# An attention and gated feed-forward kernel: the first queries and keys by SyncE and ScalarE as f32, x in column halves, one global order

## The chip, the cores and the metric

The kernel runs on one core of a Trainium2 chip. The metric is device time in microseconds for one launch. Before the change it is 263.78 us, the median of three runs (263.61 to 264.4).

## The reference

Causal attention over 4 batches, 8 heads, 768 tokens and 64 features a head. Heads 0, 2 and 6 attend to all earlier tokens; the other five attend to the first 4 tokens and the last 64. Its output, laid out as 3,072 tokens by 512 features, is x. Then a gated feed-forward block with a gated residual:

```python
scores = (q @ k.T) / 8                  # per batch and head
scores = where(mask[head], scores, -1e9)
a = exp(scores - max); a = a / (sum(a) + 1e-9)
x = concat_heads(a @ v)                 # (3072, 512)
g = x @ w_gate                          # (3072, 1536)
ffn = (gelu(g) * (x @ w_val)) @ w_out   # (3072, 512)
out = x + sigmoid(x @ w_res) * ffn
```

All inputs and the output are f32. The kernel multiplies in f16 and sums in f32.

## The kernel before

**Tiling.** The 24 token tiles of 128 go through in six chunks of four tiles (`CHUNKS`); a chunk may hold the end of one batch and the start of the next. For each chunk:
- queries and keys come into `qks`, cast to f16 by DMAs that GpSimd issues, and are turned so that features lie on partitions (`qT`, `kT`): on TensorE for chunks 0 and 1 (`loads_rows`, L824 transposes, L835 copies out of PSUM), by DMA transposes on SyncE for the others (`loads_natural`);
- four head pairs get scores on TensorE (L1012, two heads side by side on 64 partitions each; L1103 for the four sink tokens), exp on ScalarE (L1028, L1110), a mask on VectorE (L1064), the product with the values (`va`, and `vs`, the values shifted by 64 tokens; L1136, L616), and division by the row sum (L1190, L1201, L1203), which writes x as f32 (`xtok`) and f16 (`x`);
- x is turned into `xT` (L1225 on TensorE, or a DMA transpose L1216), then gate and value products with `wg` and `wv`, gelu, and `hT`; for half of the features of chunks 1 to 5 with seven products of sub-blocks in place of eight (`fast`, L1361, L1365);
- `wr` gives the residual gate (tanh on ScalarE), `wo` the output, again with seven products in place of eight (`output_fast`, L1494); gate times product goes to `otile` (L1518). For chunks 1 to 4 x is stored first (L1443) and `otile` added to it by an accumulating DMA on GpSimd (L1522); for chunks 0 and 5 x is added on the chip (L1528, L1568) and the tile stored.

Chunk 0 is done in two halves of two tiles each. Its keys and queries of tokens 0 to 255 and of tokens 256 to 511 are the first things that the kernel needs.

**Tile modes of TensorE.** A matmul uses the whole array, or half of its columns (64 output partitions, two at a time, L617 and L824), or half of its rows (scores, L1012), or a quarter (sinks, L1103).

**Order.** `PLAN` holds a list of task numbers for each of the five engines and a buffer number for each tile. `Graph.schedule` walks the five lists through a model of durations; each engine takes only the head of its own list. PSUM banks are given by kind of use (`P_ps`: which banks a kind may have, and how many at once). Where the model's TensorE has nothing ready, it puts in a filler, a matmul of a zero tile `blank` that nobody reads (L1578); fillers are dropped once the first gate product has been placed. `assign_waits` and `emit` then write semaphores and instructions; an engine runs its instructions strictly in the order written.

**Buffers.** x has two f32 buffers of four tiles by 512 columns (`P_x`); `hT` has one.

## Time and profile before

| | |
|---|---|
| time, median of three runs | 263.78 us (263.61 to 264.4) |
| span of the profiled execution | 261.9 us |
| median less that span | 1.88 us |
| TensorE busy, granted clock | 253.3 us (97%), 0.998 |
| VectorE, ScalarE, GpSimd busy | 202.2, 169.0, 107.7 us |
| first scores start, last turn of x in chunk 0 ends | 10.34, 27.35 us |
| last matmul ends | 257.13 us |
| bytes moved by DMA | 33.18 MB, 127 GB/s over the span |

The span runs from the first to the last instruction of the profiled execution; the page gives no other time for that execution, so what lies around the span is taken as the difference to the median. A group's row reads: line, engine, operation, out<-in, count, busy time and mean of one, idle time before. In the stage table each engine has its busy time, with its number of instructions behind it. A busy TensorE is not TensorE at its peak, since each matmul's row covers its pipeline too; the starts of consecutive rows tell how fast matmuls really follow each other.

### The profile page before, as it was taken

To read this page: it belongs to the slowest core of one execution; us is meant where nothing else is said; L and a number is where in the kernel's file an instruction comes from. 1 tells how busy PE (TensorE), PEld (TensorE's weight loads), DVE (VectorE), ACT (ScalarE), POOL (GpSimd) and SP (SyncE) were. 2 spreads that over 40 slices of the span, in tenths; PEclk is the share of its full clock that TensorE was granted. 3 is DMA by queue.
4 is the path that set the end of the run, shared out by engine and by line. 5 is a ranking of instruction groups with operands and counts; after the bars stand their busy time and mean duration, and the time that the engine had idled before them with its cause. 6 is when DMAs were issued, how large, how long until landed. Compare 5 with 4: busy or idle time off the path is not lost.

```text
span 261.9 us, 8109 instructions
## 1 busy us (share of the span) xinstructions
PE 253.3 (97%) x3436; PEld 181.4 (69%) x3436; DVE 202.2 (77%) x443; ACT 169.0 (65%) x303; POOL 107.7 (41%) x146
## 2 busy tenths in 40 slices
PE   7899999999999999999999999999999998999992
PEld 5568655458577477667578577689687677788891
DVE  2587449788888987868988788978687986678974
ACT  2488537795676997467896566896465994564511
POOL 8899918970061964243998330001110040010032
PEclk9999999999999999999999999999999999999999
DMA  7999999999989999999999999607940029060003
GB/s 67 162 186 191 196 191 194 183 170 153 168 226 136 154 138 143 209 178 129 128 93 110 151 199 130 204 5 116 228 104 1 3 22 137 12 80 4 3 22 141
DMA packets 102068, 33.18 MB, mean 127 GB/s; under 512 B 88720, under 2 KB 97168, under 8 KB 102032
## 3 DMA queue, kind: packets, MB, share of 16 engines
q0 software_dynamic: 74704, 18.88, 82.4%
q1 hardware_dynamic: 27040, 13.52, 26.0%
q8 instruction: 27, 0.44, 0.8%
q10 hardware_dynamic: 288, 0.26, 0.3%
q14 instruction: 9, 0.07, 0.1%
HBM read 29.36 MB, written 10.49 MB: 152 GB/s over the span
## 4 chain that ended last, share of the span: by engine, by line
PE 93%; DMA 2%; DVE 1%; issue 1%; POOL 1%; DVEq 0%; POOLq 0%
PE ps L616 47%; PE ps L617 33%; PE ps L1012 6%; DMA qks<-in_q_dram 2%; PE ps L1136 2%; PE ps L1578 2%; PE ps L1225 2%; PE ps L824 1%; PE ps L1103 1%; POOL qks L678 1%; DVE otile L1518 0%; DVE otile L1528 0%; DVE xtok L1203 0%; DVE ea L1064 0%; DVE rcp L1190 0%
## 5 line engine op out<-in xcount | busy, mean ns | idle before, releaser
L1522 POOL DMA_DIRECT2D out_dram<-otile x16 | 14.9, 966 | 87.9 <-DVE otile L1518 65.8
L678 POOL DMA_DIRECT2D qks<-in_k_dram x37 | 31.4, 892 | 31.7 <-DMA kT<-qks 24.3
L616 PE MATMUL ps<-xT,wg 128*128 128x512 f16 (+1 forms) x172 | 38.7, 337 | 0.0
L1291 ACT ACTIVATE gact<-ps 128x512 f16<-128x512 f32 x38 | 21.9, 596 | 22.9 <-PE ps L616 14.8
L1293 DVE SCALAR_TENSOR_TENSOR hT<-gact,ps 128x512 f16<-128x512 f16 x38 | 25.9, 686 | 12.5 <-PE ps L616 6.7
L616 PE MATMUL ps<-xT,wv 128*128 128x512 f16 (+1 forms) x160 | 35.3, 334 | 0.0
L678 POOL DMA_DIRECT2D qks<-in_q_dram x37 | 31.0, 867 | 6.8 <-PE ps L824 6.8
L1365 DVE TENSOR_TENSOR ps<-ps,otile 128x256 f32<-128x256 f32 x60 | 25.0, 430 | 6.3 <-PE ps L617 2.6
L678 POOL DMA_DIRECT2D va<-in_v_dram x24 | 24.3, 1021 | 0.0
L1028 ACT ACTIVATE ea<-ps 128x1024 f16<-128x1024 f32 (+2 forms) x24 | 21.5, 917 | 3.9 <-PE ps L1012 3.7
L1383 ACT ACTIVATE gact<-ps 128x512 f16<-128x512 f32 x30 | 16.5, 594 | 10.4 <-PE ps L616 6.0
L616 PEld LDWEIGHTS ps<-xT,wg 128*128 128x128 f16 x172 | 16.6, 98 | 9.5 <-DVE hT L1293 0.4
L616 PEld LDWEIGHTS ps<-xT,wv 128*128 128x128 f16 x160 | 15.3, 98 | 10.6 <-issue 0.4
L1390 DVE SCALAR_TENSOR_TENSOR hT<-gact,ps 128x512 f16<-128x512 f16 x30 | 19.5, 682 | 3.3 <-PE ps L616 1.8
L617 PE MATMUL ps<-xT,wv 128*64 128x512 f16 (+1 forms) x168 | 20.8, 350 | 0.0
L616 PE MATMUL ps<-wo,hT 128*128 128x256 f16 (+1 forms) x114 | 18.8, 296 | 0.0
L1494 DVE TENSOR_TENSOR otile<-otile,ps 128x256 f32<-128x256 f32 x33 | 13.5, 418 | 6.7 <-PE ps L616 3.4
L1203 DVE TENSOR_TENSOR xtok<-ps,rcp 128x512 f32<-128x512 f32 (+1 forms) x28 | 17.1, 610 | 1.4 <-DVE rcp L1190 0.5
L1462 ACT ACTIVATE srs<-ps 128x512 f32<-128x512 f32 x22 | 13.2, 598 | 7.7 <-PE ps L617 6.5
L617 PE MATMUL ps<-xT,wg 128*64 128x512 f16 (+1 forms) x144 | 17.4, 344 | 0.0
L1012 PE MATMUL ps<-qT,kT 64*128 64x64 f16 (+4 forms) x391 | 16.6, 213 | 0.0
L1361 ACT ACTIVATE ps<-ps 128x256 f32<-128x256 f32 x25 | 9.2, 369 | 10.6 <-PE ps L617 6.9
(174 smaller groups left out, 597.8 us busy)
## 6 DMA issues: line engine op xcount, KB each, us to landing
out_dram<-xtok SPq DMA_DIRECT2D x4, 1024.0 KB, 5.3
out_dram<-otile POOLq DMA_DIRECT2D x16, 256.0 KB, 4.9
va<-in_v_dram POOLq DMA_DIRECT2D x24, 128.0 KB, 8.5
qks<-in_q_dram POOLq DMA_DIRECT2D x32, 64.0 KB, 5.2
qks<-in_k_dram POOLq DMA_DIRECT2D x32, 64.0 KB, 7.6
wv<-in_moe_w_val_dram POOLq DMA_DIRECT2D x3, 512.0 KB, 10.0
wg<-in_moe_w_gate_dram POOLq DMA_DIRECT2D x3, 512.0 KB, 8.1
wo<-in_moe_w_out_dram POOLq DMA_DIRECT2D x4, 384.0 KB, 19.6
```

The costliest lines, as they stand in the source:

```text
L616: return e.matmul(o, lhsT=lhsT, rhs=rhs, **k)
L617: return [e.matmul(o[h:h + 64], lhsT=lhsT[:, h:h + 64], rhs=rhs, **k) for h in (0, 64)][-1]
L678: return G.add(eng, issue, lambda e: e.dma_start(out_ap(), in_ap), deps, prio, bufs=bufs, dma=cost, name=name, grp=grp)
L1012: return [e.matmul(at(scr)[:, oo:oo + w], lhsT=side(BB, qb, low, 1)[half, k0:k0 + 128], rhs=side(BB, qb, low, 0)[half, qq:qq + w], start=T ...
L1028: return e.activation(out=o, in_=i_, func=AF.Exp, scale=SM_SCALE)
L1203: t2 = G.add("dve", c_dve(2 * n * 64), lambda e: e.tensor_tensor(out=xview(), in0=avv(0, DHEAD), in1=scale(), op=ALU.mult), [t1] + xdeps, ...
L1291: ta = G.add("act", c_act(512), (lambda gb=gb, ga=ga, gw=gw: lambda e: e.activation(out=at(ga)[:, :], in_=at(gb)[:, gw], func=AF.Gelu))(), ...
L1293: th = G.add("dve", c_dve(512), (lambda vb=vb, ga=ga, f=f, vw=vw: lambda e: e.scalar_tensor_tensor(out=hv(f), in0=at(ga)[:, :], scalar=0.5 ...
L1365: return G.add("dve", c_dve(256), lambda e: e.tensor_tensor(out=at(ps)[:, o], in0=at(ps)[:, BL], in1=at(es)[:, 0:256], op=ALU.add), deps, ...
L1383: ta = G.add("act", c_act(512), (lambda x=x, ga=ga, both=both: lambda e: e.activation(out=two(at(ga)[:, :]), in_=both(x), func=AF.Gelu))() ...
L1390: th = G.add("dve", c_dve(512), (lambda x=x, f=f, ga=ga, both=both: lambda e: e.scalar_tensor_tensor(out=two(hv(f)), in0=two(at(ga)[:, :]) ...
L1522: t = G.add("pool", 1.0, (lambda ot=ot, r0=r0: lambda e: e.dma_start(out[r0:r0 + 128, :], at(ot)[:, :], accum_op=ALU.add))(), ends + [stor ...
```

## The change

**Loads.** Queries and keys of tokens 0 to 255 no longer come as f16 through GpSimd. SyncE and ScalarE issue eight DMAs of 128 tokens by four heads as f32, into the space of `hT`, which is not in use yet; even heads first, then odd ones. TensorE turns them as f32, 16 transposes of 128 by 128 in place of 32 half transposes, with an f32 identity that VectorE makes there (`wide`), and the copies out of PSUM make f16 of them. GpSimd builds the masks first and then issues the keys of tokens 256 to 511.

**x.** Three half buffers of four tiles by 256 columns in place of two whole ones. The stores of x for chunks 1 to 4 become two each; the additions of x on the chip become two of 256 columns.

**PSUM.** Any use may have any bank or any aligned pair of banks; caps and kinds are gone. The lanes of `fast` are buffers of their own.

**Order.** `PLAN` is one list for all engines; letters say on which of several engines a task runs; `w15` means 15 fillers. There is no model of durations in the program any more. A filler is left out where no bank is free of other engines' reads. The extra edges between tasks that only shaped the order (`order=`) are gone. DMA semaphores are shared by DMAs that follow each other.

```diff
-    P_x = Pool(many("xtok", 2, [128, 4, D_MODEL], FP32))
+    P_x = Pool(many("xtok", 3, [128, 4, 256], FP32))
...
-    P_ps = Psum(psum, {
-        "av1": (3, one(0, 1, 6)), "av2": (2, [(0, 1), (4, 5), (2, 3)]),
...
+    pairs, any_ = [(4, 5), (2, 3), (0, 1), (6, 7)], one(7, 6, 5, 4, 3, 2, 1, 0)
+    P_ps = Psum(psum, {"av1": any_, "av2": pairs, "sc": pairs, "lane": pairs, "warm": any_,
+                       "scr": any_, "scr0": any_, "gv": any_, "gv0": any_, "gvh": any_, "out": any_, "fin": any_,
     })
...
+        for x in "".join(PLAN).split():
+            if x[0] == "w":
+                for _ in range(int(x[1:])):
+                    t = next(fillers)
+                    t.bufs[0].fixed = t.bufs[0].pool.quiet("warm")
+                    if t.bufs[0].fixed is not None:
+                        place(t, "pe")
+            else:
+                t = self.tasks[int(x.rstrip("padgs"))]
+                place(t, {"p": "pe", "a": "act", "d": "dve", "g": "pool", "s": "sp"}[x[-1]] if x[-1] in "padgs" else t.eng)
...
+        first = Buf(P_h) if c == 0 else None
+        wide = lambda o, w: at(first)[:, :, :, :].rearrange("p f i k -> p (f i k)").bitcast(FP32)[:, o:o + w]
+        rows = lambda j, s_, i: ((j * 2 + s_) * 2 + i) * 256
...
+                    if c == 0 and y == 0:
+                        for i in range(n):
+                            t = G.flex({on: (0.6, (lambda j=j, i=i, s_=gi, src=src: lambda e: e.dma_start(
+                                wide(rows(j, s_, i), 256).rearrange("p (h d) -> p h d", h=4),
+                                src[b, s_:NHEAD:2, lo + i * 128:lo + i * 128 + 128, :].rearrange("h p d -> p h d")))())
+                                for on in ("sp", "act")}, [], base + 4 * gi + 1 - j, bufs=[first], dma=0.5, name="hw", grp=f"hw{j}{gi}")
...
+                        if f32:
+                            return [e.transpose(out=at(scr)[:, (m * n + i) * 128:(m * n + i + 1) * 128],
+                                                in_=wide(rows(jj, p // 2, i) + p % 2 * 128, 128), identity=wide(2048, 128))
+                                    for m, (p, jj) in enumerate(items) for i in range(n)]
...
-        stored[c] = G.add("sp", 0.65, lambda e: e.dma_start(
-            out[r0:r0 + n * 128, :].rearrange("(i p) d -> p i d", p=128), at(xbuf)[:, 0:n, :]),
+        stored[c] = [G.add("sp", 0.65, (lambda y=y: lambda e: e.dma_start(
+            out[r0:r0 + 512, y * 256:y * 256 + 256].rearrange("(i p) d -> p i d", p=128), at(xbuf[y])[:, :, :]))(),
...
-            for w, deps in [(p[0], [t_]) for p, t_ in zip(parts, ends)] if end else [(slice(0, 512), ends)]:
+            for w, deps in [(p[0], [t_]) for p, t_ in zip(parts, ends)] if end else [(slice(256, 512), ends), (slice(0, 256), ends)]:
```

What TensorE computes keeps its number of matmuls and their sizes, apart from the 16 f32 transposes for 32 half ones, 24 `wr` and 24 `wv` half matmuls that become 12 whole ones each, and the fillers: 68 in the order before, 35 in the new one. Counted over the whole order of TensorE without fillers, the tile mode changes 106 times before and 93 times after; from the 32 transposes for chunk 1 to the end it is 73 and 64 times. VectorE takes over from ScalarE 17 copies of 128x256 from PSUM to `otile`, 8 from PSUM to PSUM, 4 small ones of `vk`, 3 of 128x256 into `xT`, 2 casts of x and 1 copy into `vs`; it has 484 instructions in place of 443.

**The start.** In the rows an operation has the partitions and elements that it writes. TensorE before, from its first instruction; `blank` are fillers, `ident,qks` the transposes (x16 is the keys of tokens 256 to 511, the following ones the first 256 tokens), `qT,kT` the first scores:

```order
L1578 MATMUL ps<-blank 128x256 x29
L824 MATMUL ps<-ident,qks 64x128 x16
L1578 MATMUL ps<-blank 128x256
L824 MATMUL ps<-ident,qks 64x128 x8
L1578 MATMUL ps<-blank 128x256 x2
L824 MATMUL ps<-ident,qks 64x128 x8
L1578 MATMUL ps<-blank 128x256 x3
L824 MATMUL ps<-ident,qks 64x128 x8
L1578 MATMUL ps<-blank 128x256
L1012 MATMUL ps<-qT,kT 128x128 x6
```

TensorE after; `hT` are the f32 transposes (four of even-head queries, eight of keys, four of odd-head queries):

```order
L1433 MATMUL ps<-blank 128x256 x15
L706 MATMUL ps<-hT 128x128 x4
L1433 MATMUL ps<-blank 128x256 x5
L706 MATMUL ps<-hT 128x128 x8
L709 MATMUL ps<-ident,qks 64x128 x16
L880 MATMUL ps<-qT,kT 128x128 x7
L880 MATMUL ps<-qT,kT 128x64 x2
L880 MATMUL ps<-qT,kT 128x128
L880 MATMUL ps<-qT,kT 128x64 x2
L880 MATMUL ps<-qT,kT 128x128
L1433 MATMUL ps<-blank 128x256 x7
L706 MATMUL ps<-hT 128x128 x4
```

The keys of tokens 256 to 511 still stand ahead of the first scores. Behind the last row come 8 fillers and the 16 transposes of the queries of tokens 256 to 511. From the first scores to the first gate or value product TensorE has 32 fillers before and these 15 after.

GpSimd before, from its first DMA to its first one of a weight:

```order
L678 DMA qks<-in_k_dram 128x8x128
L678 DMA qks<-in_k_dram 128x4x128
L678 DMA qks<-in_q_dram 128x4x128
L678 DMA qks<-in_k_dram 128x4x128
L678 DMA qks<-in_q_dram 128x4x128
L678 DMA qks<-in_q_dram 128x8x128
L636 ISA
L636 AFFINE_SELECT ident<-ident 128x128
L654 MEMSET m_causal 128x128
L678 DMA va<-in_v_dram 128x8x64 x2
L678 DMA wv<-in_moe_w_val_dram 128x4x512
```

GpSimd after, the same stretch from the first instruction for the identity; one more mask instruction, two more pieces of values and the first weights follow:

```order
L504 AFFINE_SELECT ident<-ident 128x128
L527 MEMSET m_win 128x256
L504 AFFINE_SELECT m_win<-m_win 128x256
L522 MEMSET m_causal 128x128
L504 AFFINE_SELECT m_causal<-m_causal 128x128
L504 AFFINE_SELECT m_win<-m_win 128x256
L546 DMA qks<-in_k_dram 128x8x128
L504 AFFINE_SELECT m_win<-m_win 128x64
L546 DMA va<-in_v_dram 128x8x64 x2
L532 MEMSET m_win 128x64
L546 DMA qks<-in_q_dram 128x8x128
```

The four loads of the first 256 tokens have left GpSimd, and its one load of keys now stands behind six instructions for the identity and the masks, and the last mask instruction follows the load of the second queries. ScalarE issues one of the eight f32 DMAs, then loads its table of functions, then issues three more; SyncE issues its four at once.

VectorE after, from its first instruction of work (`hT<-ident` is the f32 identity; the first `kT` row is one half of the even-head keys):

```order
L519 MEMSET ident 128x64
L518 MEMSET blank 128x128
L541 MEMSET va 128x48
L539 MEMSET vk 128x520
L658 CAST hT<-ident 128x128
L515 COPY m_win<-m_win 128x256
L720 CAST kT<-ps 128x2x256
L723 COPY kT<-ps 128x2x256
```

Before, the copy of the window mask `m_win` stood behind the copies of the keys and queries of the first half; now it is ahead of both copies of keys.

**Scores of the fourth chunk on TensorE**, which run between the third chunk's last gate products (`xT`, `wr`) and its output products (`wo`, `wt`); before:

```order
L616 MATMUL ps<-wr,xT 128x512 x4
L1103 MATMUL ps<-qT,kT 32x384 x4
L1103 MATMUL ps<-qT,kT 32x128 x8
L617 MATMUL ps<-xT,wv 64x512 x8
L617 MATMUL ps<-wr,xT 64x512 x8
L1012 MATMUL ps<-qT,kT 128x64 x16
L616 MATMUL ps<-wo,hT 128x256 x6
L1012 MATMUL ps<-qT,kT 128x128 x8
L616 MATMUL ps<-wt,hS 128x256 x7
```

and after:

```order
L486 MATMUL ps<-wr,xT 128x512 x4
L971 MATMUL ps<-qT,kT 32x384 x4
L971 MATMUL ps<-qT,kT 32x128 x8
L486 MATMUL ps<-wo,hT 128x256 x6
L880 MATMUL ps<-qT,kT 128x64 x16
L486 MATMUL ps<-wt,hS 128x256 x7
```

Between sinks and scores stands one stretch in another mode where two stood (half columns, 64x, are a mode of their own), and the following block of scores comes later.

**The end.** VectorE's last instructions before; `srs` is the gate, the last row adds x to a whole tile:

```order
L1494 TENSOR_TENSOR otile<-otile,ps 128x256 x2
L1518 SCALAR_TENSOR_TENSOR otile<-srs,otile 128x512
L1528 TENSOR_TENSOR otile<-otile,xtok 128x256
L1518 SCALAR_TENSOR_TENSOR otile<-srs,ps 128x256
L1518 SCALAR_TENSOR_TENSOR otile<-srs,otile 128x256
L1528 TENSOR_TENSOR otile<-otile,xtok 128x512
```

and after:

```order
L1350 TENSOR_TENSOR otile<-otile,ps 128x256 x2
L1374 SCALAR_TENSOR_TENSOR otile<-srs,otile 128x512
L1384 TENSOR_TENSOR otile<-otile,xtok 128x256
L1374 SCALAR_TENSOR_TENSOR otile<-srs,otile 128x256
L1374 SCALAR_TENSOR_TENSOR otile<-srs,ps 128x256
L1384 TENSOR_TENSOR otile<-otile,xtok 128x256
```

The gate of the half that does not need the last product comes first, and VectorE adds x to one half alone; GpSimd has five additions of 256 columns in its order in place of three and one of 512.

414 lines of the change are left out of this document (125 added, 289 removed), and 158 rows, old and new, of tables (PLACES, PLAN).

## Prediction

> **What bounds the kernel now.** I read the page first: the slices and the chain of waits.
>
> ```profile
> span 261.9 us, 8109 instructions
> PE   7899999999999999999999999999999998999992
> DMA  7999999999989999999999999607940029060003
> PE 93%; DMA 2%; DVE 1%; issue 1%; POOL 1%; DVEq 0%; POOLq 0%
> ```
>
> TensorE holds 93% of the chain, is full from the second slice to the last but two, and no other engine holds more than 2%. So only three things can shorten the run: the time until TensorE has real work, what TensorE loses between matmuls, and the end behind its last matmul. The stage table, cut at the first transposes, the first scores, the first value product, the last turn of x in chunk 0 and the last matmul (PE, PEld, DVE, ACT, POOL, clock, DMA share, GB/s), gives their sizes:
>
> ```profile
> 0.00:6.86 6.86, 5.15 (x29) 3.70 (x30) 1.42 (x6) 1.49 (x2) 5.67 (x13) 1.00 0.74 71
> 6.86:10.33 3.47, 2.86 (x47) 1.78 (x47) 1.39 (x3) 1.19 (x2) 3.40 (x7) 1.00 1.66 159
> 10.33:20.87 10.54, 10.53 (x184) 7.10 (x184) 9.00 (x26) 8.78 (x19) 9.63 (x18) 1.00 1.67 178
> 20.87:27.35 6.48, 6.48 (x118) 5.49 (x116) 5.13 (x18) 5.25 (x9) 6.48 (x9) 1.00 1.38 200
> 27.35:257.13 229.78, 228.30 (x3064) 163.35 (x3061) 183.43 (x389) 152.32 (x272) 81.57 (x104) 1.00 1.08 123
> 257.13:261.90 4.77, 0.00 (x0) 0.00 (x0) 1.86 (x3) 0.00 (x0) 0.99 (x1) 0.89 0.37 137
> ```
>
> 229.78 us are the dense part, 27.35 the start, 4.77 the end. The clock is full, so it is no lever. TensorE looks busy in the start too, but not with work; the group row for fillers and the timeline say so:
>
> ```profile
> L1578 PE MATMUL ps<-blank 128*128 128x256 f16 x68 | 11.8, 312 | 1.1 <-DVE blank L650 1.1
> 1.13 5.15 PE L1578 MATMUL ps<-blank 128*128 128x256 f16 x29 [1.13 <-DVE blank L650]
> 1.35 1.88 POOL L678 DMA_DIRECT2D qks<-in_k_dram  x2 [0.84 <-POOLq L1662]
> 10.34 0.46 PE L1012 MATMUL ps<-qT,kT 64*128 64x128 f16 x14
> 11.07 0.94 PE L1578 MATMUL ps<-blank 128*128 128x256 f16 x7
> 12.02 0.64 PE L824 MATMUL ps<-ident,qks 128*64 128x128 f16 x16
> 20.71 0.60 PE L616 MATMUL ps<-xT,wv 128*128 128x256 f16 x4
> ```
>
> 11.8 of the first 27.35 us are fillers. The first 29 run 5.15 us (0.178 each); later ones follow each other every 0.107 (the same x256 columns as a half-column pair of x512). Real work begins at 6.9, scores at 10.34, value products at 20.71.
>
> **The start (term S).** What matters there is when data lands:
>
> ```profile
> 0.00:3.00 3.00, 1.87 (x9) 1.35 (x10) 1.42 (x6) 1.49 (x2) 1.85 (x6) 1.00 0.00 0
> 4.00:10.00 6.00, 4.82 (x63) 3.28 (x61) 1.29 (x2) 1.15 (x2) 5.88 (x10) 1.00 1.63 158
> 0.81 1.28 ACT L1580 ACT_TABLE_LOAD   x1 [0.81 <-PEq L1662]
> qks<-in_k_dram POOLq DMA_DIRECT2D x1, 256.0 KB, 4.8
> qks<-in_q_dram POOLq DMA_DIRECT2D x3, 256.0 KB, 6.4
> out_dram<-otile ACTq DMA_DIRECT2D x2, 128.0 KB, 1.8
> wv<-in_moe_w_val_dram POOLq DMA_DIRECT2D x3, 512.0 KB, 10.0
> L636 POOL TENSOR_SCALAR_AFFINE_SELECT m_win<-m_win 128x256 f16<-128x256 f16 (+1 forms) x4 | 1.3, 329 | 0.3
> L678 POOL DMA_DIRECT2D va<-in_v_dram x3 | 2.8, 935 | 0.0
> ```
>
> The DMA engines move nothing for 3 us and then 158 GB/s; loads from GpSimd take 4.8 to 6.4 us from issue to landing, a quiet hardware DMA of 128 KB 1.8. SyncE and ScalarE can issue from 0.8 on, so the even-head queries land at about 2.7 to 3.3 and stand ready when the 15 fillers end (1.13 + 15 x 0.178 = 3.8). Half of the even-head keys stand behind ScalarE's table load of 1.28 and a first activation, with one DMA ahead of it: issued at about 2.7, landed at 5 to 7 by the two kinds of row, 1.8 and 4.8.
>
> That does not set the first scores, though. In TensorE's order the keys of tokens 256 to 511 stand ahead of them, and GpSimd issues those behind six instructions of about 0.33: 1.15 + 2.0 = 3.2, plus 4.8 gives 8.0, plus 0.64 for the transposes. The change also adds a wait: VectorE's copy of the window mask waits for GpSimd's last mask instruction, which now follows the load of the second queries (3.2 + 0.9 + 0.25 + 2 x 0.935 + 0.2 + 0.9 + 0.25 = 7.6). Behind that copy (some 0.5) stands the copy of the even-head keys (0.7), and the scores wait for it: 8.8. I take 8.8, 1.5 before the 10.34 of now.
>
> Then come the scores (0.4), 7 fillers (0.75), four f32 transposes, 8 fillers (0.85). No row shows an f32 transpose; between the 0.055 that an f16 one of x128 takes at the rate of the x256 filler and four times that, I take the upper end, 0.9 for four. That is 11.7. But the second queries are issued at 6.4 and land at 12.8 by their row: 0.8 later than the 12.02 of now. From there to the value products it takes 8.7 us now, of which 25 fillers are 2.7; 6.0 remain. VectorE (9.00) and ScalarE (8.78) leave only 1.5 to 1.8 of 10.54 free, so a part of what fillers covered stays as a wait; I add 1.0. 12.8 + 6.0 + 1.0 = 19.8 against 20.71: **S = -0.9**. The value weights, issued at 9.4 with 10.0 to landing, come at 19.4, just in time.
>
> Lower end: the queries land in 4.8 and nothing waits, 11.7 + 6.0 = 17.7: -3.0. Upper end: the eight f32 DMAs carry 1.05 MB, twice the bytes that the casting loads wrote; at 158 GB/s that is 6.6 us, to 9.3, shared with the second keys and queries. They land some 2 us later, and the weights with them at 21.4: products at 22.2, +1.5. This is a rule of the Trainium skill too: "DMA: Bandwidth & Descriptors", section "Issuing engines are not separate DMA queues", says that DMAs of all three issuers run on the same 16 engines and that spreading the issue saves only issue time. By it S would be the upper end; the trace here has no hardware load beside a GpSimd load in the start, but it does show the engines empty for 3 us, which is the part that an earlier issue can win even so.
>
> **Tile modes (term M).** A change of mode costs time that the busy share hides; starts of consecutive rows show it:
>
> ```profile
> 254.22 1.05 PE L617 MATMUL ps<-wr,xT 128*64 128x512 f16 x8
> 255.08 0.52 PE L617 MATMUL ps<-wo,hT 128*64 128x256 f16 x6
> 128.15 1.03 PE L617 MATMUL ps<-wr,xT 128*64 128x512 f16 x8
> 129.11 0.41 PE L1012 MATMUL ps<-qT,kT 64*128 64x64 f16 x16
> 129.45 0.83 PE L616 MATMUL ps<-wo,hT 128*128 128x256 f16 x6
> ```
>
> Eight half-column matmuls take 0.86 when the same mode follows, 0.96 when scores follow: 0.10 for the change. Sixteen scores of 64 columns, two side by side, need 16 x 0.0134 = 0.21 at the rate of these rows (0.1075 per x512) and take 0.34: 0.13. From chunk 1 on the changes go from 73 to 64. **M** = -9 x 0.12 = **-1.1**, on TensorE's path, hidden by nothing. Ends: -1.5, and -0.5 if the blocks that now stand together wait for exp. `wr` and `wv` as whole or half columns take the same time, so those cost nothing.
>
> **A gap in fetching or issue (term I).**
>
> ```profile
> 220.97 0.19 PE L1136 MATMUL ps<-vs,es 128*64 128x65 f16 x1 [1.24 <-issue]
> ```
>
> In the middle of 16 window products, between instructions that wait for nothing, TensorE stands for 1.24. No semaphore explains it, so it depends on where an instruction happens to stand; in another order it may vanish or come back. Ends -1.24 and 0; I take **I = -0.9**, since it is one such gap in 230 us.
>
> **The end (term T).**
>
> ```profile
> 256.27 0.85 PE L617 MATMUL ps<-wt,hT 128*64 128x256 f16 x12
> 257.22 0.42 DVE L1518 SCALAR_TENSOR_TENSOR otile<-srs,ps 128x256 f32<-128x256 f32 x1 [0.23 <-PE ps L617]
> 257.56 0.83 DVE L1518 SCALAR_TENSOR_TENSOR otile<-srs,otile 128x256 f32<-128x256 f32 x1
> 258.43 0.69 DVE L1528 TENSOR_TENSOR otile<-otile,xtok 128x512 f32<-128x512 f32 x1
> ```
>
> Behind the last matmul three VectorE instructions end at 259.12. In the new order the gate that needs only the last tanh comes first (0.42), then the last product's (0.42), then one addition of 256 columns (0.42), while GpSimd adds the other half: 257.13 + 0.1 + 1.26 = 258.5. **T = -0.6**; -1.0 if the first gate is done before the last matmul, -0.2 if GpSimd's addition slows a gate to 0.83 again.
>
> **Moved work.** VectorE takes 36 operations from ScalarE: 17 + 8 copies of 0.42, the rest 3.2, in all 13.7 us.
>
> ```profile
> L1488 DVE COPY otile<-ps 128x256 f32<-128x256 f32 x6 | 2.5, 420 | 0.8 <-PE ps L617 0.8
> 240.00:250.00 10.00, 10.00 (x158) 8.81 (x156) 9.17 (x19) 5.02 (x12) 0.00 (x0) 1.00 0.01 2
> ```
>
> I cost it at nothing: VectorE is busy 183.43 of the dense 229.78 us, so 46 are free. Halved x buffers, twice as many stores and freer banks cost nothing by the same cover: stores and SyncE are idle for tens of us in the late slices. Without the cover it is the slower rival below.
>
> **Sum.** 261.9 - 0.9 - 1.1 - 0.9 - 0.6 = 258.4 of span; the median lies 1.88 above the span (263.78 - 261.9), so **260.3 us**.
>
> **Rivals.**
> - *The start comes forward as a whole* (S = -3.0, other terms as above): 258.2. For it: 17 fillers fewer between scores and value products, and empty DMA engines in the first 3 us. Against: ScalarE and VectorE near 85% there.
> - *The loads come late* (S = +1.5): 261.9 + 1.5 - 2.6 + 1.88 = 262.7. For it: 158 GB/s is all that the start shows and the f32 loads double the bytes; against: the empty 3 us.
> - *The same work in another order*: the gap returns elsewhere, fewer mode changes are paid with waits for exp, S and T with waits for weights: 263.8, no change. For it: TensorE's matmuls are the same in number and size.
> - *VectorE becomes the bound* (the slower side): in the last stretches it is at 9.17 of 10. If half of the 13.7 us falls where it has no room, TensorE waits for its merges and masks: 260.3 + 6.9 = 267.2. It decides from 4.3 us exposed on. Against: 46 us free.
>
> **Chances.** Forecast 0.45 (own range 259.2 to 261.6), forward start 0.20, late loads 0.15 (0.09 of it below the bound), same work 0.08, VectorE 0.12. A measurement here tells 0.3% from no change, 263.0 to 264.6. Faster: 0.45 + 0.20 + 0.09 = 0.74; same 0.06 + 0.08 + 0.01 = 0.15; slower 0.11. The range from 257.4 to 264.2 reaches below the forward start by 0.8, room for T's and I's lower ends, takes in late loads and unchanged, and leaves out VectorE and a little on the low side.
>
> **What would show it.** First scores at 8.8 and value products near 19.8 (S); at 17.7 the forward start, at 22 the late loads, with 158 GB/s or less while waiting. Dense part shorter by 2.0: mode changes still 0.10 to 0.13 each, no gap over 1 us without a releaser (M, I). Last matmul to last addition 1.4 in place of 2.0 (T). Waits of TensorE for VectorE in the dense part, or VectorE over 9.5 of 10 in several stretches, would make the forecast wrong; so would an f32 transpose well over 0.22.

## The result: 1.2% slower

The changed kernel takes 268.76 us, median of ten runs (264.89 to 270.71), against 263.59 (263.19 to 264.65) for the kernel before, run beside it. The ratio is 1.0121, with a 95% interval of 1.0072 to 1.0169. (Ratios here leave out runs that lie over 1.5% above the fastest of their kernel; medians are of all runs.) By the medians of all runs it is 2.0%. The forecast was 260.3 and faster: it was wrong in its sign, and the time lies above its range.

The profiled execution took 269.4 us with a span of 267.5, 5.6 more than before. It is one of the longer ones of the ten, so what follows explains more than the ratio asks for; a second profile of the same program (c1, 271.25 us) shows the same two losses. Its page, first lines, slices and chain of waits:

```profile
span 267.5 us, 7978 instructions
PE   7879999999999999999999699999999999999991
PEclk9997999999999999999999799999999999999998
PE 76%; DVE 10%; DMA 9%; POOL 2%; issue 1%; POOLq 0%; ACT 0%; DVEq 0%; ACTq 0%
```

Two things are new. TensorE has a slice of 6 a little past the middle, and the clock has two slices of 7, one in the start and one at that same place. TensorE's share of the chain fell from 93% to 76%. The stage table of the changed kernel, cut at the same events as that of before, has its numbers (28.12 is where the last turn of x in chunk 0 starts; it ends at 28.40):

```profile
0.00:4.38 4.38, 3.17 (x15) 2.32 (x16) 0.92 (x5) 1.49 (x2) 3.20 (x12) 1.00 0.58 122
4.38:9.69 5.31, 3.79 (x35) 2.74 (x35) 0.83 (x2) 1.19 (x2) 5.31 (x9) 1.00 1.76 190
9.69:20.00 10.31, 8.51 (x169) 6.05 (x166) 8.20 (x26) 8.50 (x18) 9.56 (x15) 1.00 1.64 189
20.00:28.12 8.12, 8.12 (x119) 6.37 (x114) 6.34 (x23) 5.21 (x8) 6.51 (x8) 0.79 1.32 205
28.12:261.99 233.87, 229.76 (x3039) 164.54 (x3036) 194.14 (x426) 137.26 (x238) 78.87 (x100) 0.99 1.03 120
261.99:267.50 5.51, 0.00 (x0) 0.00 (x0) 1.77 (x4) 0.00 (x0) 1.70 (x2) 0.86 0.26 97
```

First scores and value products come earlier (9.69 and 20.00 for 10.34 and 20.71), and then 20 to 28 is run at a clock of 0.79. In the dense part TensorE is busy 229.76 of 233.87 us, where it had been busy 228.30 of 229.78: it waits. The waits of TensorE name for whom (us in total, times, longest):

```profile
PE ps L486 <- DMA xT<-x: 2.6, 1, 2.6
PE ps L487 <- DMA xT<-x: 0.6, 1, 0.6
PE ps L487 <- DVE ps L1228: 0.5, 1, 0.5
```

It is one wait, for the half of x of the fourth chunk that SyncE turns. Windows of the changed kernel around the start's slow stretch and behind that wait show what comes with it (clock, DMA share and GB/s are the last three columns):

```profile
15.00:20.00 5.00, 3.35 (x73) 2.20 (x72) 4.87 (x18) 3.81 (x8) 4.42 (x6) 1.00 1.45 196
20.00:25.00 5.00, 5.00 (x72) 3.80 (x69) 3.67 (x15) 2.37 (x4) 4.33 (x6) 0.66 1.38 203
147.50:150.10 2.60, 0.04 (x1) 0.00 (x1) 0.02 (x1) 0.00 (x0) 2.60 (x4) 0.97 1.30 121
150.10:152.00 1.90, 1.90 (x5) 0.73 (x6) 1.50 (x4) 0.60 (x1) 1.90 (x3) 0.50 2.70 154
152.00:153.00 1.00, 1.00 (x4) 0.45 (x3) 0.05 (x1) 0.60 (x1) 0.42 (x1) 0.50 1.20 207
153.00:154.00 1.00, 1.00 (x7) 0.59 (x6) 0.64 (x1) 0.37 (x1) 0.00 (x0) 0.82 1.57 160
```

After each of the two idle stretches TensorE runs at half clock for a while: 0.34 x 5 = 1.7 us are lost in 20 to 25, and 0.95 + 0.50 + 0.18 = 1.6 us in 150.1 to 154. Before, the clock was 1.00 throughout the start.

To say where the 5.6 us arose, I added up in both traces the matmuls done, without fillers (columns times the share of the array in use), and compared the moments at which the same amount of work was finished:

| stretch of the changed kernel | later than before by |
|---|---|
| start to the end of the first chunk | +0.6 (of it 1.7 from half clock) |
| 28 to 147 us | -0.4 |
| 147 to 160 us | +4.3 (wait 2.6, half clock 1.6) |
| 160 us to the last matmul | +0.4 |
| behind the last matmul (5.51 for 4.77) | +0.7 |

So the questions for experiments were: what makes x's half late, what lets the clock fall, and whether VectorE (the slower rival of the prediction) is behind it.

### The profile page after: what moved, and what is told of

The parts are those of the page before. It is cut to its first block, busy times and chain, and to the rows that moved or that the text cites. A ratio compares the mean times of both kernels' runs of the same rounds, so it can differ in the third digit from the quotient of the medians.

```text
span 267.5 us, 7978 instructions
## 1 busy us (share of the span) xinstructions
PE 253.4 (95%) x3363; PEld 182.0 (68%) x3363; DVE 212.2 (79%) x484; ACT 153.7 (57%) x268; POOL 105.1 (39%) x143
## 4 chain that ended last, share of the span: by engine, by line
PE 76%; DVE 10%; DMA 9%; POOL 2%; issue 1%; POOLq 0%; ACT 0%; DVEq 0%; ACTq 0%
PE ps L486 44%; PE ps L487 23%; DMA xT<-x 4%; PE ps L880 4%; DMA out_dram<-otile 3%; DMA qks<-in_k_dram 2%; DVE hT L1251 2%; PE ps L1004 1%; PE ps L709 1%; DVE hS L1272 1%; PE ps L1093 1%; DVE otile L1374 1%; PE ps L1433 1%; DVE otile L1350 1%; DVE x L1070 1%
## 5 line engine op out<-in xcount | busy, mean ns | idle before, releaser
L1378 POOL DMA_DIRECT2D out_dram<-otile x16 | 15.7, 1018 | 79.1 <-DVE otile L1350 34.3
L486 PE MATMUL ps<-xT,wg 128*128 128x512 f16 (+1 forms) x172 | 39.9, 346 | 2.6 <-DMA xT<-x 2.6
L486 PE MATMUL ps<-xT,wv 128*128 128x512 f16 (+1 forms) x172 | 41.2, 347 | 0.0
L546 POOL DMA_DIRECT2D qks<-in_k_dram x35 | 30.4, 896 | 7.7 <-DMA kT<-qks 7.7
L486 PEld LDWEIGHTS ps<-xT,wv 128*128 128x128 f16 x172 | 16.8, 100 | 10.3 <-issue 1.1
L487 PE MATMUL ps<-xT,wg 128*64 128x512 f16 (+1 forms) x144 | 18.1, 344 | 1.1 <-DMA xT<-x 0.6
L487 PE MATMUL ps<-xT,wv 128*64 128x512 f16 (+1 forms) x144 | 18.2, 344 | 0.0
L487 PE MATMUL ps<-wo,hT 128*64 128x256 f16 x216 | 16.0, 273 | 0.0
```

Of the source, the lines that this page charges most:

```text
L486: return e.matmul(o, lhsT=lhsT, rhs=rhs, **k)
L487: return [e.matmul(o[h:h + 64], lhsT=lhsT[:, h:h + 64], rhs=rhs, **k) for h in (0, 64)][-1]
L546: return G.add(eng, issue, lambda e: e.dma_start(out_ap(), in_ap), deps, prio, bufs=bufs, dma=cost, name=name, grp=grp)
```

## The experiments

All kernels compute the whole reference. `PLAN` is a list of task numbers, so most edits move numbers; "..." stands for what lies between. The last column is (1 - granted clock) x span, the time lost to a lower clock, as a mean over all runs; the kernel before has 0.4 to 0.9 by this measure (in its profile above, 0.5, all of it behind the last matmul).

| run | median (range, runs), us | ratio to before, 95% | clock loss, us |
|---|---|---|---|
| the change, first measurement | 268.76 (264.89 to 270.71, 10) | 1.0121 (1.0072 to 1.0169) | 3.3 |
| c1, the change again | 269.91 (268.00 to 273.32, 6) | 1.0191 (1.0143 to 1.0240) | 5.0 |
| c2, SyncE's order | 269.51 (265.77 to 278.12, 6) | 1.0142 (1.0089 to 1.0196) | 4.4 |
| c3, fillers | 270.28 (268.64 to 271.41, 6) | 1.0232 (1.0194 to 1.0271) | 3.8 |
| c4, c2 and c3 and the end | 269.23 (267.65 to 272.83, 6) | 1.0189 (1.0151 to 1.0226) | 3.4 |
| d1, SyncE earlier | 270.41 (266.09 to 277.06, 4) | 1.0147 (1.0079 to 1.0215) | 3.5 |
| d2, d1, one store, fillers, end | 267.38 (266.45 to 269.71, 6) | 1.0166 (1.0121 to 1.0212) | 1.6 |
| d3, before with fewer fillers | 265.28 (262.51 to 269.89, 10) | 1.0032 (0.9990 to 1.0074) | 2.4 |
| d4, copies back to ScalarE | 270.17 (267.99 to 274.31, 5) | 1.0240 (1.0183 to 1.0297) | 5.5 |
| e1, loads ahead | 266.34 (264.12 to 270.18, 8) | 1.0081 (1.0049 to 1.0114) | 3.6 |
| e2, more loads ahead, d2's edits | 269.04 (265.78 to 271.93, 6) | 1.0147 (1.0093 to 1.0200) | 3.3 |
| f1, e1, fillers, end | 267.21 (263.44 to 272.92, 11) | 1.0056 (1.0006 to 1.0106) | 2.1 |
| f2, f1, SyncE, one store | 267.87 (266.00 to 270.34, 6) | 1.0116 (1.0069 to 1.0162) | 2.0 |
| g, next chunk's loads late | 269.56 (266.70 to 271.00, 6) | 1.0196 (1.0138 to 1.0254) | 3.7 |
| g, with e1, fillers, end | 266.27 (264.90 to 271.43, 12) | 1.0085 (1.0052 to 1.0119) | 1.4 |
| h, x and stores first | 271.41 (263.63 to 271.92, 4) | none | 3.5 |
| h, with e1, fillers, end | 265.64 (262.47 to 266.90, 12) | 1.0026 (0.9990 to 1.0063) | 0.8 |

**c1: the change again**, no edit.

> The changed kernel once more, unaltered, as the base for the runs beside it. In its first profiled execution TensorE stood 2.6 us for the transposed x of the fourth chunk (row at 150.10) and then ran at half clock, matmuls of 512 columns following each other every 0.427 us in place of 0.213. If the place of SyncE's transposes alone makes this stall (theory Q), it is in every execution: a stall of 2 to 3 us near 147 and a time of 265 to 271, median near 268.8. If it was one unlucky execution (rival: disturbed transfers), the stall is under 0.5 us here and the median near 265. In both cases the clock in the stretch from 20 to 25 us is under 0.8 if the dropped fillers are its cause (theory C).

1.0191, a larger ratio than the first measurement's, with overlapping intervals. Two waits of TensorE in its profile:

```profile
PE ps L486 <- DMA xT<-x: 4.4, 1, 4.4
PE ps L487 <- issue: 1.2, 1, 1.2
```

The wait for x is there again and longer, and half clock comes again too, from 18.4 and from 151.5 us. The second row matters for the term on the gap: the program that shows no such gap in one execution has one of 1.2 us in the next.

**c2: x's half ahead of two transposes on SyncE.** SyncE's own queue, of before and then of the change, shows the suspect (transposes of queries and keys, and x's):

```profile
140.16 1.39 SPq L1216 DMA_TRANSPOSE xT<-x  x1
141.60 1.65 SPq L868 DMA_TRANSPOSE qT<-qks  x1
```

```profile
136.26 1.20 SPq L756 DMA_TRANSPOSE kT<-qks  x1
137.57 3.10 SPq L756 DMA_TRANSPOSE qT<-qks  x2
140.72 3.10 SPq L756 DMA_TRANSPOSE kT<-qks  x2
143.87 1.27 SPq L756 DMA_TRANSPOSE qT<-qks  x1
145.18 1.31 SPq L1084 DMA_TRANSPOSE xT<-x  x1
```

Before, x's half goes ahead of the queries and keys; in the change it follows six of them. VectorE had cast it by 142.54, so it stood 2.64 us behind them, about the 2.56 for which TensorE waits. (The chain of waits names VectorE's copy into `xT` there, which ends at the same moment; in c1 that copy ends at 145.42 and SyncE issues at 147.60, again right behind its sixth transpose, so the queue it is.)

The queue is only half of the delay, though. x itself was ready later than before; VectorE's last write of this half, before and then in the change:

```profile
139.39 0.69 DVE L1201 TENSOR_TENSOR x<-ps,rcp 128x512 f16<-128x512 f32 x1
```

```profile
142.12 0.42 DVE L1078 CAST x<-xtok 128x512 f16<-128x512 f32 x1
```

It ends at 140.08 before and at 142.54 in the change, while by equal work TensorE is only 0.2 us later at 147. So 2.46 of the 5.02 us by which SyncE issues x's half later (145.18 for 140.16) lie ahead of SyncE. No edit here was aimed at that part.

```diff
-    "... 1189 375 1201 ... 1204 378 1135 ... 1145 1194 388 ..."
+    "... 1189 1201 ... 1204 1135 ... 1145 1194 375 378 388 ..."
```

> The changed kernel with one edit: on SyncE the transpose of x for the fourth chunk stands ahead of the last two of the six transposes of queries and keys behind which it waited (it was issued at 145.18, while x was ready at 142.54). Theory Q (SyncE's queue): it is issued at about 142.6, lands at about 147.4, TensorE's stall there falls from 2.6 to under 0.5 us and the half clock behind it is gone: 3 to 4.5 us less than the unaltered kernel in its profile, median 264 to 265.5, and less spread. Rival V (VectorE bound by the 13.7 us of moved work): x is then late for another reason, the stall stays above 1.5 us and the time within 1 us of the unaltered kernel. Rival D (the transfer itself is slow): issue moves, landing doesn't, no gain.

1.0142: no gain that the intervals can tell. The wait for x fell to 1.33, and another came behind it. TensorE and ScalarE in the timeline of c2:

```profile
150.32 1.04 PE L486 MATMUL ps<-xT,wg 128*128 128x512 f16 x4 [1.33 <-DMA xT<-x]
158.06 0.38 ACT L1224 ACTIVATE otile<-ps 128x256 f32<-128x256 f32 x1 [3.91 <-DMA out_dram<-otile]
159.03 0.39 PE L486 MATMUL ps<-xs,wg 128*128 128x256 f16 x2 [2.26 <-DVE ps L1228]
```

ScalarE waits 3.91 us for an `otile` that an accumulating store on GpSimd has yet to free; VectorE's sum waits for ScalarE, and TensorE for VectorE. In this execution SyncE began its transposes only at 139.75 and issued x's half at 145.70, later than in the first profile of the change, so the wait did not fall because x landed earlier. What c2 shows is that a second wait, for GpSimd's queue, stands right behind the first.

**c3: the fillers that the change leaves out.** The change drops a filler if every free bank was last read by another engine than TensorE. Here it goes to the free bank whose last such reader lies longest back; 12 more are placed.

```diff
-        return next((i for i, x in enumerate(spots) if not self.busy & set(x) and
-                     all(u.eng == "pe" for b in x for u in self.last[b])), None)
+        free = [i for i, x in enumerate(spots) if not self.busy & set(x)]
+        return min(free, key=lambda i: max((u.late for u in self.last[spots[i][0]] if u.eng != "pe"), default=-1), default=None)
...
+            t.late = len(order)
```

> The changed kernel with one edit: the 12 fillers that its order asks for between the second scores and the first value products, and that are left out because no bank is free of other engines' readers, are placed all the same, in the free bank whose reader lies furthest back. Theory C (too little work on TensorE from 15 to 20 us lets the granted clock fall): the clock from 20 to 25 us returns from 0.66 to above 0.95, the last turn of x in the first chunk ends 1.0 to 1.7 us earlier, the time is 0.7 to 1.7 us less than the unaltered kernel's. Rival (my prediction's reading, fillers only cost time): 12 fillers cost up to 12 x 0.107 = 1.3 us and the clock falls as before; the time is the same or up to 1.3 us more.

The start did as expected. The same two windows in c3:

```profile
15.00:20.00 5.00, 4.79 (x84) 3.15 (x79) 4.84 (x19) 4.01 (x8) 4.51 (x7) 1.00 1.44 196
20.00:25.00 5.00, 5.00 (x91) 3.94 (x90) 4.93 (x19) 3.51 (x5) 4.19 (x6) 1.00 1.38 203
```

TensorE is busy 4.79 of 5, the clock stays at 1.00, and by equal work the first chunk ends 0.72 us ahead of the kernel before instead of 0.60 behind it. Yet the time is no better: TensorE now waits 4.66 for x's half in place of 2.6, and half clock follows there. What the start wins is lost at x: VectorE had cast it by 141.36, 1.2 us earlier than in the change, and SyncE issued it at 146.79, 1.6 us later, right behind its sixth transpose.

**c4: c2, c3 and the end's additions on VectorE.**

```diff
+    (c2's and c3's edits)
-    "... 1833g ... 1838g ..."
+    "... 1833d ... 1838d ..."
```

> The two edits before together, and a third at the end: VectorE does the last two additions of x that GpSimd did (they start behind the gates, GpSimd took 0.96 us for the last and slowed a gate from 0.42 to 0.94). If the stall for x, the clock and the end are the three losses and independent, this has 3 to 4.5 + 0.7 to 1.7 + 0.5 us less than the unaltered kernel: median 261.5 to 263.3, no slower than the kernel before (263.6) and, if the terms M and I of the prediction came true, 0.5 to 2 us faster. If VectorE is the bound (rival V), it stays above 265.

1.0189; waits for VectorE's sum 2.8 and for x 0.9. The end did improve on the change. The last instructions of the change, and then the last of c4:

```profile
261.76 0.96 POOL L1384 TENSOR_TENSOR otile<-otile,xtok 128x256 f32<-128x256 f32 x1 [1.63 <-DVE otile L1374]
262.06 0.94 DVE L1374 SCALAR_TENSOR_TENSOR otile<-srs,otile 128x256 f32<-128x256 f32 x1
262.93 0.41 DVE L1374 SCALAR_TENSOR_TENSOR otile<-srs,ps 128x256 f32<-128x256 f32 x1
263.42 0.96 POOL L1384 TENSOR_TENSOR otile<-otile,xtok 128x256 f32<-128x256 f32 x1 [0.69 <-DVE otile L1374]
```

```profile
262.37 0.42 DVE L1375 SCALAR_TENSOR_TENSOR otile<-srs,otile 128x256 f32<-128x256 f32 x1
263.15 0.76 DVE L1385 TENSOR_TENSOR otile<-otile,xtok 128x256 f32<-128x256 f32 x2
```

GpSimd takes 0.96 for an addition, and VectorE's gate beside it 0.94 instead of 0.42. With all on VectorE the end behind the last matmul is 4.84 us, against 5.51 in the change and 4.77 before: level with before, and not the 0.6 shorter that was forecast.

**d1 and d2: SyncE's transposes in the order in which their loads are issued**, and for d2 one accumulating store ahead of a load that stands, with c3's edit and c4's end.

```diff
-    "... 353 ... 356 ... 1189 375 ... 1204 378 ... 1206 382 ... 1213d 1125 ..."
+    "... 375 353 ... 378 356 ... 1189 ... 1204 ... 1206 1125 382 ... 1213d ..."
```

(`1125` moves in d2 alone.)

> The changed kernel with SyncE's transposes in the order in which their loads are issued: the two of the six that stood last before the transpose of x (their loads are the first that GpSimd issues for that batch) come first and third now. Behind the swap of the runs before, GpSimd's load that waits for one of the other transposes came later (it stood 8 us), and with it the accumulating stores behind that load; here those transposes are not moved back. Theory Q (the order on SyncE makes x late): x's transpose is issued 1.5 to 2.5 us earlier than without the edit, TensorE's wait for it falls below 1.5 us, time 266 to 268. Theory L (GpSimd's queue as a whole runs late, and SyncE only hands that on): the sum of TensorE's waits between 140 and 160 us stays 3 to 5 us, only under another name (accumulating stores that free otile), time 268 to 270, as unaltered.

> The edit on SyncE, one on GpSimd (the accumulating store that is ready at 139 us goes ahead of the load that stands 8 us for SyncE's transposes, instead of behind it), the 12 fillers and the end on VectorE together. Theory Q/L at this place only: the 5 us that TensorE waits between 140 and 160 us fall to under 1.5, start as in the run with fillers (1.3 to 2 us ahead of the unaltered kernel): 262 to 265. If the time stays above 267, the lateness of GpSimd's loads comes from further up (its waits from 27 to 85 us) and reordering at 140 us can't mend it.

1.0147 and 1.0166. Both divide the one wait into several: in d1 2.0 for x, 1.8 for VectorE's sum and 1.3 for `qT`; in d2 1.8, 1.2 and 1.4, and an issue gap of 1.1. None of the orders of SyncE that were tried removes the lateness alone.

**d3: the kernel before with 17 of its 32 later fillers left out**, so that 15 remain, as many as the change has. This asks of the clock alone.

```diff
+        first = next(i for i, t in enumerate(pe) if t.name.startswith("sc"))
+        gone = set([t for i, t in enumerate(pe) if t.name == "warm" and i > first][15:])
...
+        prog["pe"] = [t for t in pe if t not in gone]
```

> The kernel before, with the last 17 of its 32 fillers between the first scores and the first gate or value product left out, so that it has 15 there as the changed kernel has. Nothing else moves. Theory C (the clock falls where TensorE has too little to do): the granted clock falls below 0.9 somewhere between 17 and 27 us and the last turn of x in the first chunk ends 0.3 to 1.5 us later, time 264 to 265.3. Rival (fillers only cost time): clock 1.0, the start is up to 1.0 us earlier, time 262.6 to 263.6.

1.0032, an interval that just holds 1. The same two windows, of before and then of d3:

```profile
15.00:20.00 5.00, 5.00 (x79) 3.40 (x77) 4.43 (x17) 4.29 (x8) 5.00 (x7) 1.00 1.67 176
20.00:25.00 5.00, 5.00 (x89) 4.09 (x86) 3.92 (x14) 4.79 (x8) 5.00 (x7) 1.00 1.50 190
```

```profile
15.00:20.00 5.00, 3.80 (x67) 2.39 (x66) 3.91 (x15) 4.50 (x9) 5.00 (x8) 0.83 1.73 177
20.00:25.00 5.00, 5.00 (x53) 3.85 (x55) 2.81 (x11) 2.90 (x4) 5.00 (x7) 0.50 1.47 188
```

Without fillers the clock falls in the old kernel too, and its first chunk ends 1.53 us later. The clock varies from run to run: two of ten executions kept it at 1.000 and took 262.51 and 262.95, while the longest had 0.981 and 269.89. So the fillers help to hold the clock; leaving them out loses on average 1.5 us of clock (2.4 against 0.9).

**d4: 40 copies given back to ScalarE** (all copies of its kinds that the change lets VectorE do).

```diff
-    "... 797d ... 818d ... 819d ... 870d ..."
+    "... 797a ... 818a ... 819a ... 870a ..."
```

> The changed kernel with all 40 copies out of PSUM for the sub-block products (some 16.8 us) on ScalarE, none on VectorE: VectorE falls from 212 to about 195 us, ScalarE rises from 154 to about 169, as in the kernel before. Rival V of the prediction (the moved work on VectorE is the cause): 3 us or more less than the unaltered kernel, 264 to 266.5. Theory L (queues of GpSimd and SyncE): within 1.5 us of the unaltered kernel, 268 to 270.5, with the waits for x's transpose or for the accumulating stores between 140 and 160 us as before.

1.0240: no faster, and if anything slower than the change. VectorE as the bound would have shown a gain, so that rival falls as far as these copies go.

**e1: loads ahead of a load that stands.** GpSimd issues all loads but the first ones, and its queue runs strictly in order. Three windows of 28 to 60 us: before, the change, e1 (GpSimd's busy time and instructions are the fifth group; GB/s the last column).

```profile
28.00:60.00 32.00, 32.00 (x308) 17.59 (x306) 21.55 (x44) 21.24 (x35) 22.62 (x30) 1.00 1.77 184
```

```profile
28.00:60.00 32.00, 32.00 (x316) 17.75 (x313) 23.39 (x48) 17.83 (x30) 10.82 (x14) 1.00 1.56 167
```

```profile
28.00:60.00 32.00, 32.00 (x313) 17.73 (x312) 23.22 (x48) 17.90 (x30) 16.91 (x23) 1.00 1.83 183
```

In the change GpSimd issues 14 instructions in these 32 us, where before it issued 30. It stands at the head of its queue for a buffer that is not free. GpSimd's timeline of the change, and then one row of before:

```profile
42.24 1.49 POOL L546 DMA_DIRECT2D qks<-in_q_dram  x2 [15.06 <-PE ps L709]
63.32 1.77 POOL L546 DMA_DIRECT2D va<-in_v_dram  x2 [10.26 <-PE ps L1004]
84.78 1.49 POOL L546 DMA_DIRECT2D qks<-in_q_dram  x2 [13.75 <-DMA qT<-qks]
```

```profile
73.51 0.75 POOL L678 DMA_DIRECT2D qks<-in_k_dram  x1 [16.11 <-DMA kT<-qks]
```

The kernel before stands as long, only later, when more of its loads are out. e1 puts the 12 loads whose buffers are free ahead of the one that stood until 42.24, and the one load of values that stood until 63.32 behind ten others:

```diff
-    "... 269 276 ... 579 291 ... 615 281 ... 594 300 ... 596 297 ... 697 295 ... 680 280 ... 592 282 ..."
+    "... 269 291 300 297 295 301 292 294 298 281 280 282 279 276 ..."
-    "... 656 312 ... 274 602 ..."
+    "... 656 ... 274 312 602 ..."
```

> The changed kernel with GpSimd's loads regrouped at the two places where it stood 15 us (27 to 42) and 10 us (53 to 63) for a load whose buffer TensorE still reads: twelve loads whose buffers are free (eight of queries and keys, four of values) go ahead of the first one, and the one load of values behind the ten loads that stood behind it. Nothing else moves. Theory L (loads issued late run late to the end, since the DMA engines have no room to catch up): by 60 us GpSimd has issued some 10 loads more, by 90 us 15.2 MB or more are moved (14.85 in the unaltered kernel, 15.33 in the one before), SyncE's transposes of the last chunks come earlier and TensorE's waits between 140 and 160 us fall from 3 to 5 us to under 2: 265 to 267.5. If the transposes wait for their buffers anyway (rival: the chain from 70 us on sets the pace), the bytes by 90 us stay under 15.0 MB and the time within 1 us of the unaltered kernel (269 to 270).

266.34 and 1.0081. This interval lies below that of c1 (from 1.0143 on) and overlaps that of the first measurement; it is the lowest ratio of any single edit, though the change was not measured again beside it. The windows show the 28 to 60 stretch at 183 GB/s, as before the change (184), and the wait for x falls to 0.91 with SyncE's order untouched.

How the earlier loads bring this about is not shown. The expectation asked for 15.2 MB or more by 90 us; e1 moved 166 GB/s in these 90 us, which is 14.9 MB, the change 165 and the kernel before 170. From 28 to 130 us the change and e1 are level, at 157 GB/s:

```profile
28.00:130.00 102.00, 101.82 (x1013) 65.36 (x1012) 85.08 (x186) 63.21 (x110) 47.48 (x61) 1.00 1.35 157
28.00:130.00 102.00, 101.75 (x1010) 65.39 (x1007) 84.95 (x185) 63.06 (x110) 47.31 (x62) 1.00 1.37 157
```

The load that stands until 84.78 in the change stands until 83.81 in e1, and SyncE starts its six transposes at 135.60 in place of 136.26. c1, the change itself, has 86.15 and 138.65, so one execution of each can't tell e1's gain from the spread.

**e2: five more loads ahead of two accumulating stores**, with d2's edits.

```diff
+    (e1's and d2's edits)
-    "... 991 912 ... 1007 376 ... 995 373 ... 1043 409 ... 1035 408 ... 1060a 399 ..."
+    "... 991 376 373 409 408 399 912 ..."
```

> That regrouping (and five more loads ahead of two accumulating stores at 115 us that wait for VectorE), with the edits on SyncE and GpSimd at 140 us, the 12 fillers and the end on VectorE. By theory L and C the losses add: against the run with the same edits but without the regrouping (267.4) the waits from 140 to 160 us (4.5) fall to about 1: 263 to 265, and if also its start is 0.7 us ahead as in the run with fillers alone, 262 to 263.5, as the kernel before or a little faster. If it stays above 266.5, something other than the loads' lateness holds the middle.

1.0147: little of what e1 won is left, though the intervals overlap. GpSimd's store in the change, and then the store, VectorE and TensorE in e2:

```profile
114.60 1.79 POOL L1378 DMA_DIRECT2D out_dram<-otile  x2 [8.44 <-DVE otile L1374]
```

```profile
120.39 1.84 POOL L1379 DMA_DIRECT2D out_dram<-otile  x2
126.14 0.42 DVE L1226 COPY otile<-ps 128x256 f32<-128x256 f32 x1 [7.19 <-DMA out_dram<-otile]
127.16 0.61 PE L487 MATMUL ps<-xs,wv 128*128 128x256 f16 x2 [6.24 <-DVE ps L1229]
```

The loads took the stores' place and stood there 11.93 us for a buffer: the stores left 5.8 us later, VectorE waited 7.19 for the tile that they free, TensorE 6.24. Loads and stores share one queue, so an early load can cost as much as a late one.

**f1: e1, c3 and the end. f2: f1 with SyncE's order of d1 and one store of d2.**

```diff
+    (f1: the edits of e1 and c3, and c4's end)
+    (f2: those, and d2's moves of 375, 378 and 1125)
```

> The changed kernel with the twelve loads and the one of values regrouped on GpSimd (the run that came to 266.3), the 12 fillers, and the end on VectorE; GpSimd's accumulating stores and SyncE stay as they are. In the run before, five loads moved ahead of two accumulating stores stood for their buffers and made the stores 5.8 us later, and TensorE stood 6.2 us for them: that edit is left out. If the three losses add, 266.3 - 1.3 (clock at 20 us) - 0.7 (end) = 264.3, between 263 and 265.5. If lateness on GpSimd comes back because TensorE asks 1.4 us earlier (theory L says the loads' time, not TensorE's, sets 140 to 160 us): the waits there grow by as much, and the gain is the end alone: 265.6.

> The same with SyncE's transposes in the order of their loads and the one accumulating store ahead of the load that stands for SyncE at 139 us. By theory L these two free the last 1 to 2 us of waits from 140 to 160 us: 262.5 to 264.5, at least as fast as the kernel without them. If they cost (as the five loads did), more than 265.5.

f1 is at 1.0056, apart from c4 (from 1.0151 on), which has no loads moved but also c2's edit on SyncE; f2 is at 1.0116, overlapping f1. The row at which TensorE resumes behind x's half, of e1 and then of f1:

```profile
148.69 1.04 PE L486 MATMUL ps<-xT,wg 128*128 128x512 f16 x4 [0.91 <-DMA xT<-x]
```

```profile
148.65 1.04 PE L487 MATMUL ps<-xT,wg 128*128 128x512 f16 x4 [2.20 <-DMA xT<-x]
```

f1 kept its clock in the start and TensorE came 1.3 us earlier to this place, yet resumed at the same time, 148.65 for 148.69. Here x's landing sets the time, not TensorE, as in c3.

**g: loads of the sixth chunk behind those of the fifth, and SyncE's keys first**; then the same with e1, c3 and the end.

```diff
-    "... 1043 409 ... 1035 408 ... 387 1158 ... 353 1122 ... 1181 343 ... 1189 375 ..."
+    "... 1043 ... 1035 ... 387 409 408 399 400 405 406 402 1158 ... 353 343 375 1122 ..."
```

> The changed kernel with GpSimd's seven loads of queries and keys that only the sixth chunk needs moved behind the loads of the fifth chunk, among which they stood from 117 to 135 us, and SyncE's three transposes of keys ahead of its three of queries (the queries' buffer is read by TensorE's scores until 136). If the order makes the wait between 140 and 160 us: the fifth chunk's loads land 4 to 5 us earlier, SyncE begins near 131 to 133 in place of 136, x's transpose is issued within 1 us of x being ready (142.5), TensorE's waits there fall from 3 to 5 us to under 1.5, 265 to 267. If the DMA engines have no room: the loads land at the same time as before whatever their order, waits stay over 3 us, 268.5 to 270.

> That, with the regrouping of GpSimd's loads at 27 and 53 us, the 12 fillers and the end on VectorE. If order is the cause and the clock holds, the waits at 140 to 160 us are gone and the 0.9 us of lead at 120 us (as in the run with regrouping, fillers and end) reaches the end: 262 to 263.3, faster than the kernel before by 0.2 to 0.6%. If there is no room: 265 to 267, as without it.

1.0196 and 1.0085. The loads were moved, but GpSimd then stood from 117.5 to 123.8 for SyncE's transposes of queries, and SyncE's first transpose came at 135.84 in place of 136.26. With e1's edits the result is e1's. Moving the sixth chunk's loads did not help.

**h: x's transpose behind three of the six on SyncE, and three accumulating stores ahead of the loads that stand**; then with e1, c3 and the end.

```diff
-    "... 1181 343 ... 1189 375 ... 1204 378 ... 1206 382 ... 1194 388 ... 362 ... 397 ... 403 ... 1157 ... 348 ..."
+    "... 1194 343 375 378 ... 1157 382 388 362 397 403 348 ..."
```

> The changed kernel with x's transpose third on SyncE, behind three of the six transposes (the kernel before has it ahead of all of them), and three accumulating stores on GpSimd ahead of the load that stands 8 us for SyncE at 138 us. If what stands ahead in these two queues is the cause: x's transpose is issued within 0.5 us of x being ready, the stores leave as soon as VectorE is done, TensorE's waits between 140 and 160 us fall from 3 to 5 us to under 1, and 266 to 267 (the clock at 20 us and the end still cost). If a new wait comes (scores of the fifth chunk for queries and keys, at 165 to 180 us), it is 1 to 2 us: 267.5 to 269.

> That with the regrouping of loads at 27 and 53 us, the 12 fillers and the end on VectorE. Lead at 120 us 0.9 us, as in the run with regrouping, fillers and end; if it reaches the end: 262 to 263.3, faster than the kernel before by 0.2 to 0.6%. If waits of the fifth chunk's scores take it: 264 to 266.

The first alone gave no ratio (three of its four runs lay at 271). In its profile x's half is issued at 145.23, only 0.67 us after its cast, and yet TensorE waits 2.96 for it: the place in SyncE's queue is not all.

Together with the rest it took 265.64 and 1.0026 (0.9990 to 1.0063), below both measurements of the change. The interval holds 1; by the medians of all runs it is still 1.8 us above the kernel before. TensorE's two longest waits between 140 us and the end are 1.4 for x's half and 1.1 for a copy of keys (`q`). Its clock loss is 0.8, that of the kernel before. It differs from the change in order, in 12 fillers and in the engine of the last two additions alone; the f32 loads, the half buffers, the free banks and VectorE's moved work are all still there. So most of the cost of the change lies in its order and its fillers. No version beat the kernel before.

## Why the prediction was wrong, step by step

**The failed step** is the last one of the moved work: "Halved x buffers, twice as many stores and freer banks cost nothing by the same cover: stores and SyncE are idle for tens of us in the late slices". Idle time in the late slices covers nothing in the middle, and the sum held no term at all for what the new order does there. In its place the trace shows x's half of the fourth chunk cast 2.46 us later than before, then issued by SyncE behind six transposes instead of ahead of them, a wait of 2.56 us, and half clock behind it: +4.3 us between 147 and 160 in the profiled execution. GpSimd's queue takes part (14 instructions in place of 30 between 28 and 60 us, and a lower ratio when its loads are moved, e1), in a way that stays open. What the half buffers, the doubled stores and the freer banks cost by themselves no run shows; h with e1, c3 and the end keeps all three and comes to 1.0026. The order of the change could be read ahead of time for exactly these two engines; the prediction looked there only at TensorE, VectorE and the start.

**S, forecast -0.9, came out at -0.7 by the first value products, as it was counted, and at +0.6 by the end of the first chunk**, since half clock followed. The events were right: products at 20.00 (forecast 19.8), second queries' transposes at 12.31 (12.8), scores at 9.69 (8.8; TensorE waits 1.28 for the keys of tokens 256 to 511), f32 transposes 0.213 each (the upper end taken). Late loads did not come: the stretch of 4.38 to 9.69 moved 190 GB/s, more than the 158 of before, and the first 10 us 159 GB/s in place of 98. The rule of the Trainium skill that was weighed ("DMA: Bandwidth & Descriptors", "Issuing engines are not separate DMA queues") would have had the three issuers win only issue time; the trace shows the earlier issue and 20% more rate, though with other DMAs in flight. What failed is that fillers were counted as a cost alone: the forecast added 1.0 for waits where fillers had been, and the clock lost 1.7 on top. The sum has no term for that. c3 and d3 show it from both sides.

**M, forecast -1.1, came out at -0.9.** Mode changes behind the first chunk fell from 74 to 65 in the traces, and the delay summed over them (from the last start in one mode to the first in the next, less the time of the former's columns) from 9.1 to 8.3 us.

**I, forecast -0.9, can't be credited.** The gap of 1.24 is absent in this profile of the change, but c1, the same program, has one of 1.2, and d2 and g have gaps of 1.1 to 2.0. It differs between executions of one program, so the order alone doesn't set it.

**T, forecast -0.6, came out at +0.7.** The bound of "-0.2 if GpSimd's addition slows a gate" had the gate right (0.94 for 0.42) and forgot that the last addition itself may be GpSimd's, 0.96 behind the last gate. With VectorE it is +0.1 (c4: 4.84), so the 0.6 did not come there either.

**Moved work at no cost** is borne out for the copies (d4), 25 of the operations that VectorE took over (35 by the list ahead of the prediction, not 36). The others, two casts of x among them, no run gave back.

**The rivals.** VectorE as the bound had a time, 267.2, near the result, but d4 speaks against its mechanism, and TensorE's waits for VectorE in the dense part are 0.7. Forward start and late loads did not occur. "The same work in another order" held a piece of the truth, fewer mode changes paid for with waits, though it priced the waits as an even exchange. What was missing among the rivals is one on the order of a queue in the middle of the run, and one on the clock.

**Shown and open.** Shown by runs: that most of the loss lies in the order and the fillers (h with e1, c3 and the end against both measurements of the change); the fillers that hold the clock in the start (c3, d3); the store behind loads (e2); the end (c4); and by issue times in the traces of the change, c1 and c3 that x's half stood behind six transposes. Shown by ratios alone: that GpSimd's loads moved ahead help (e1 beside c1; f1 beside c4, which differs by c2's edit too). Open: how the loads' order reaches the time; why x is cast later, and what is left of the loss when SyncE issues it at once (h alone); why SyncE's transposes ahead of it begin anywhere between 130.4 and 139.8 us; and why single executions of one program differ by 5 us.

## What to carry to other kernels

When a new order is predicted, follow every in-order queue through the whole run, the ones that issue DMAs first: for each load or store, ask what stands ahead of it and for which buffer that waits. A gain upstream was worth nothing where the next meeting point was set by data on another queue (c3, f1). And fillers do work if they hold the clock: cost their removal by the half-clock stretch behind it (1.7 us here), not by their own time alone.
